# Turning the tokens' normalised rows by one DMA of four blocks instead of four TensorE transposes

## The chip, the core and the metric

The kernel runs on one core of one Trainium2 chip. The core has TensorE (PE in the profile, with PEld for its weight loads), VectorE (DVE), ScalarE (ACT), GpSimd (POOL) and SyncE (SP), which in this kernel issues nearly all DMAs. The engines run side by side, each with its own list of instructions that it takes strictly in order; they wait for each other by semaphores. The metric is the device time of one execution in microseconds (us); the kernel before has a median of 1510.49 us over 3 runs (1509.76 to 1510.58).

## The reference

Four layers follow each other on 2048 tokens of 448 features: attention with memory, a gated unit, the same attention with the same weights again, the same gated unit again.

```python
x = A_x
x = x + _A_ref(_layernorm(x), A_mem0, A_Wq, A_Wk, A_Wv, A_Wo, A_seg_len)
x = x + _B_ref(_layernorm(x), B_W_gate, B_W_up, B_W_down)
x = x + _A_ref(_layernorm(x), A_mem0, A_Wq, A_Wk, A_Wv, A_Wo, A_seg_len)
x = x + _B_ref(_layernorm(x), B_W_gate, B_W_up, B_W_down)

# _A_ref: 16 heads of 256; segments of 32 tokens, 8 memory rows in front of each
mem = mem0
for s in range(n_seg):                       # 64 segments, one after the other
    h = concat([mem, xs])                    # 40 rows
    q, k, v = h @ Wq, h @ Wk, h @ Wv
    p = softmax(where(mask, q @ k.T / 16, -1e9))
    o = (p @ v) @ Wo
    mem = o[:8]                              # the next segment's memory
    outs.append(o[8:])

# _B_ref
gate = x @ W_gate
out = (gate * (gate > 0) * (x @ W_up)) @ W_down
```

The memory makes a chain: a segment's 8 memory rows come out of the whole attention of the segment before it.

## The kernel before

**Weights.** Wq and Wk of a head are multiplied once into a matrix A (`self.A`, 448 x 448 a head), and Wv with Wo into B (`self.Bsb`). A score is then `h A h^T`, and the output `p h B`. TensorE spends about the first 118 us on that.

**Tiles, steps, layers.** Tokens are worked on in 16 tiles of 128 (four segments each). Each of the two attention layers (layer 0 and layer 1 in the code) has 64 segments. `program` runs over steps: at step `n`, `chain(n)` carries the memory rows of layer 0 from segment `n` to `n + 1`, and those of layer 1 from segment `n - 7` (`LAG`) on; both ride through the same matmuls. Up to two times eight query rows of layer 1's even tiles ride along too (`board` copies them into the chain's operand `mT`). Between the chain's parts, `tiles` lets TensorE do the rest of a tile's work: `att_group` four times (the matmuls with A, L1626; scores, L1655; softmax; `p h`, L1537 and L1541; B, L1693), then `glu_units` (L1715) and `glu_down` (L1733), for layer 0 and for layer 1.

**One step of the chain.** Matmuls with A (L1268), evictions into `Usb`, turning with a selection matrix (L1444), scores (L1467), softmax on ACT and DVE, the turn of P on TensorE into `PTm` (L1507), `p h` (L1534), evictions into `YTm`, matmuls with B (L1307), four partial sums added by ACT and DVE (L1322, L1324 twice, L1325) into `Ohi`, a small copy (L1205), and the turn of the new memory rows by matmuls with a selection (L1350), whose evictions fill `mT` for the next step.

**The rows that the change is about.** `norm(t, ("A", l))` makes a tile's normalised rows `xn` (128 tokens by 448 features): statistics (L1556, L1557), two small ACT operations (L1558, L1560), the scaling (L1562) and a copy of the first 64 features (L1205, in `twice`). Matmuls need these rows with the features on the partitions. 448 is three and a half times 128, so there are four blocks, the last of them holding 64 features twice. TensorE turns the four blocks (L1580) into one PSUM bank. From there one copy makes `HT`, where each segment's 32 columns have 8 more for its memory (stride 40), and two copies make `HX`, which holds the first three blocks with their halves of 64 partitions exchanged: the matmuls with A (L1626) work on 64 rows at a time, two side by side, and each side takes seven half blocks, four from `HT` and three from `HX`. The same norm issues eight small DMAs that put the rows, not turned, into `HR` (24 KB and 4 KB pieces). `HT`, `HX` and `HR` have two buffers for layer 0 and three for layer 1 (`NB`). For the gated unit (`norm(t, "G")`) the rows are turned by two DMAs from SBUF to SBUF already, of three and of four blocks (`turn_dma`, L1046), and softmax results of the tiles and of the riders as well.

**The order.** No scheduler runs at build time: `ORDER` is one long list, found by a search outside of this file, that holds each operation's number times five plus the number of its engine; each engine takes its operations in the list's order. `BANKS` gives the PSUM bank of each use. `FILLS` names places in that list at which TensorE gets matmuls without a use ("fillers", L183): number, bank, and shape. Each of them may start once `s.still` (a cleared tile, `warm`) is there.

```python
FILLS = {56: (11, 0, 0), 69: (9, 0, 0), 1306: (7, 2, 0), 1461: (46, 1, 1)}
```

Of the kernel before, what the change touches and what calls it, by code (L numbers as in the profile page):

```python
# [7 lines left out]
ALU = mybir.AluOpType  # L8
# [8 lines left out]
SEG = 32  # L17
# [267 lines left out]
def bass_interleave_layers__memory_aug_recurrent_mem_tr__glu_gated_reglu__prompt_kernel(  # L285
# [22 lines left out]
    206, 2, 8, 199, 211, 204, 22, 142, 78, 12, 226, 219, 138, 148, 231, 224, 246, 239, 17, 251, 244, 27, 32, 58,  # L308
    37, 153, 92, 266, 259, 42, 158, 102, 163, 47, 112, 271, 264, 275, 52, 168, 122, 290, 62, 173, 281, 639, 67, 178,
    297, 183, 539, 188, 286, 302, 193, 72, 305, 82, 2128, 544, 87, 320, 2133, 311, 549, 327, 316, 554, 332, 335, 559, 355,  # L310
    341, 564, 362, 569, 435, 643, 405, 574, 441, 420, 412, 669, 450, 446, 417, 426, 345, 674, 457, 385, 431, 462, 351, 879,
    495, 392, 525, 884, 501, 485, 532, 889, 375, 491, 365, 894, 382, 395, 371, 465, 899, 402, 515, 471, 904, 475, 522, 505,
    909, 481, 605, 512, 914, 95, 790, 611, 2167, 590, 1179, 797, 620, 616, 1184, 596, 105, 775, 2172, 802, 627, 575, 1189, 2176,
    632, 760, 601, 782, 2181, 1194, 581, 115, 645, 745, 2187, 652, 1199, 657, 2193, 586, 662, 751, 767, 735, 2204, 675, 772, 741,
    787, 695, 2209, 757, 682, 705, 701, 2214, 825, 2162, 712, 815, 2219, 831, 2157, 865, 2257, 821, 2224, 725, 872, 715, 731, 2229,
    805, 2262, 722, 2266, 845, 2234, 811, 685, 852, 2271, 2239, 855, 691, 2277, 835, 1204, 861, 960, 2282, 842, 1209, 1060, 966, 1075,
    1214, 1067, 1045, 971, 1072, 1081, 945, 1479, 1052, 1090, 951, 1057, 930, 1087, 1097, 915, 936, 1102, 957, 1115, 922, 1155, 941, 927,
    1121, 1484, 1125, 1162, 1105, 1559, 1131, 975, 1112, 1135, 981, 1165, 1142, 1005, 1171, 995, 1012, 1035, 1001, 1025, 1042, 1015, 1031, 1145,
    1022, 985, 1151, 1390, 1564, 992, 125, 1230, 1396, 132, 1639, 1375, 1237, 1260, 1401, 1242, 1381, 1515, 1267, 1360, 1386, 1272, 1525, 1366,
    1485, 1345, 1371, 1535, 1351, 1495, 1644, 1542, 1215, 1356, 1505, 1719, 1221, 1492, 1245, 1565, 1226, 1252, 1501, 1575, 1257, 1585, 1571, 1512,  # L320
    1435, 1521, 1582, 1445, 1531, 1295, 1442, 1591, 1625, 1452, 1301, 1405, 1415, 1411, 1724, 1305, 1422, 1285, 1799, 1311, 1455, 1292, 1335, 1461,
    1275, 1342, 1315, 1281, 1465, 1322, 1325, 1471, 1425, 1332, 1545, 1431, 1705, 1804, 1552, 2345, 1879, 2350, 2285, 2356, 2362, 1605, 2331, 1595,
    1612, 2195, 1601, 1735, 2242, 1665, 2336, 2247, 1745, 2252, 1741, 1615, 2342, 1645, 1884, 1751, 1622, 1675, 1651, 1959, 2365, 1632, 1681, 2370,
    1695, 2376, 2382, 2385, 1655, 2391, 1765, 1661, 1685, 1772, 1805, 1671, 1964, 1855, 1811, 1692, 1775, 2039, 1701, 1815, 1782, 1925, 1711, 1822,
    1935, 2395, 1905, 2401, 1835, 1911, 2405, 1825, 1842, 1941, 1755, 2412, 1915, 1831, 1725, 1861, 2415, 2044, 1865, 1732, 1945, 2139, 2422, 1871,
    1762, 2025, 2426, 2144, 1785, 1952, 1985, 2149, 1791, 2432, 2118, 2437, 2015, 1991, 2154, 1885, 1975, 2021, 2294, 1892, 2005, 1981, 2032, 1845,
    2299, 1921, 2440, 1965, 2012, 2123, 2304, 2446, 1895, 1851, 1972, 1995, 2309, 1901, 2055, 2002, 2314, 1931, 2045, 2062, 2065, 2319, 2051, 2075,
    2072, 2324, 2085, 2081, 4157, 2095, 2329, 2105, 2091, 2102, 2559, 2450, 2111, 4162, 2457, 2569, 2461, 3365, 6062, 4166, 3370, 2579, 4171, 4177,
    2465, 2584, 4182, 6067, 6071, 6076, 2490, 2471, 2564, 2477, 2483, 2574, 2487, 3375, 2496, 2589, 3380, 2502, 2594, 2505, 3386, 2510, 2515, 2522,
    2527, 2599, 2605, 3391, 2532, 2537, 2541, 2625, 2549, 2630, 2554, 2610, 2636, 2642, 3395, 2616, 2622, 2824, 2655, 2645, 2819, 2661, 2665, 3400,  # L330
    2651, 2672, 2829, 2675, 3405, 2682, 2604, 2686, 3530, 3412, 3535, 2692, 3417, 3426, 2697, 3421, 3432, 2700, 3540, 3437, 2706, 2710, 2839, 3545,
    2716, 2722, 3551, 2725, 2834, 3556, 2750, 2731, 2737, 2849, 2743, 2747, 2844, 3560, 2756, 3565, 2762, 2765, 2770, 2775, 2781, 2786, 2859, 2865,
    2791, 2797, 2801, 2870, 2809, 2885, 2814, 2876, 2882, 2854, 2890, 3079, 3570, 2896, 2902, 3695, 3576, 2905, 3084, 3581, 3592, 2915, 3586, 2925,
    3700, 2912, 2921, 2932, 2864, 3596, 3601, 2935, 3705, 2942, 3089, 2946, 3710, 2952, 3094, 3725, 2957, 3716, 3722, 2960, 3730, 2966, 2970, 3099,
    3735, 2976, 2982, 3741, 3757, 3104, 2985, 3746, 3762, 3751, 3767, 3010, 2991, 2997, 3109, 3003, 3007, 3860, 3016, 3025, 3022, 3030, 3035, 3041,
    3046, 3145, 3051, 3057, 3061, 3150, 3069, 3125, 3074, 3156, 3162, 3114, 3130, 3440, 3136, 3142, 3175, 3605, 3447, 3181, 3452, 3165, 3185, 3612,
    3865, 3171, 3192, 3457, 3195, 3617, 3870, 3461, 3202, 3622, 3206, 3875, 3467, 3626, 3212, 3890, 3472, 3119, 3217, 3881, 3477, 3220, 3632, 3895,
    3484, 3886, 3227, 3637, 3230, 3642, 3900, 3236, 3242, 3906, 3922, 3649, 3270, 3911, 3927, 3916, 3932, 3359, 3245, 3276, 3124, 3282, 3364, 3485,
    3251, 5510, 3491, 3257, 3263, 3267, 3496, 3650, 5516, 5522, 3500, 3285, 3290, 3506, 3770, 3339, 3657, 3301, 3295, 3306, 3512, 3311, 4275, 3321,
    3662, 3316, 3777, 4295, 3329, 3782, 3787, 3334, 4280, 3791, 3797, 4300, 4286, 4292, 3344, 3665, 3802, 4306, 4312, 4315, 3935, 3671, 4322, 3515,  # L340
    3807, 3676, 4248, 3942, 3814, 3947, 4253, 4335, 3952, 4258, 4325, 3520, 4342, 3956, 4263, 4332, 4999, 3962, 4268, 3967, 4273, 4345, 3525, 3972,
    5004, 4352, 4356, 3979, 3680, 4362, 4367, 4370, 3685, 3349, 4376, 4380, 3830, 4386, 4392, 3815, 3837, 3841, 4395, 3821, 3827, 4420, 4401, 3354,
    4407, 4413, 4417, 3690, 4426, 4432, 4435, 4440, 3980, 4451, 4456, 3995, 3987, 4194, 4485, 4461, 4471, 3991, 4002, 4199, 4490, 4006, 4204, 4505,
    4496, 4502, 4209, 4510, 4214, 4445, 4516, 4522, 4219, 3845, 4466, 4224, 4525, 4479, 4545, 4535, 4531, 3850, 4552, 4541, 4484, 4229, 4555, 3855,
    4562, 4566, 4010, 4572, 4577, 4580, 4015, 4586, 4590, 5385, 4596, 4602, 4605, 5391, 5407, 5396, 5412, 5401, 5417, 4630, 4611, 4617, 4623, 4627,
    4020, 4636, 4642, 4645, 4650, 4027, 4655, 4661, 4666, 4695, 4671, 4032, 4676, 4682, 4037, 4715, 4041, 4689, 4046, 4052, 4700, 4694, 4057, 4720,
    4064, 4706, 4712, 4726, 4732, 4735, 4741, 4069, 4745, 4755, 4185, 4751, 4762, 4231, 6082, 4765, 5370, 4772, 6088, 4236, 4776, 4242, 4782, 4787,
    4790, 5525, 5376, 5382, 4796, 4800, 5531, 5547, 4070, 8334, 4806, 4812, 5536, 5552, 5541, 5557, 4840, 4076, 4082, 4815, 4846, 4852, 8337, 8342,
    4085, 4821, 8346, 4827, 4833, 8351, 4837, 4130, 4091, 4097, 4855, 4860, 4100, 4871, 4876, 4881, 4891, 5012, 5560, 4106, 5420, 4112, 4115, 5427,
    5567, 4135, 5432, 4121, 5572, 5437, 4127, 5441, 4140, 5577, 5447, 5581, 5452, 4145, 5587, 5457, 5665, 4152, 5464, 5592, 4907, 5650, 5597, 5671,  # L350
    4912, 5687, 4916, 5604, 5676, 5692, 4921, 5697, 5681, 4927, 4865, 5656, 4932, 4944, 5662, 4935, 4886, 5790, 4949, 4982, 4987, 5018, 4899, 4992,
    4904, 5007, 5023, 5465, 5796, 5802, 5025, 4954, 5471, 5477, 4959, 5030, 4964, 5045, 5036, 5042, 4969, 5050, 4974, 5480, 5056, 5062, 6153, 5105,
    4979, 6158, 5700, 5486, 5112, 5069, 5115, 5491, 5125, 5707, 5605, 5122, 5620, 5611, 5805, 5132, 5616, 5627, 5631, 5712, 5135, 5717, 5811, 5495,
    5827, 5816, 5721, 5142, 5822, 5146, 5727, 5500, 5151, 5157, 5831, 5167, 5836, 5162, 5172, 5732, 5175, 5840, 5737, 5181, 5744, 5185, 5847, 5505,
    5191, 5197, 5071, 5077, 5082, 5200, 5852, 5089, 5857, 5861, 5867, 5225, 5872, 5206, 5877, 5212, 5884, 5217, 5635, 5222, 5252, 5231, 5237, 5640,
# [464 lines left out]
class _Kernel:  # L820
# [153 lines left out]
    def constants(self):  # L974
# [9 lines left out]
        def dve(fn, **k):  # L984
            s.add("dve", 250, lambda E, e: fn(E), **k)
# [875 lines left out]
```

## Time and profile before

| what | value |
|---|---|
| median of 3 runs | 1510.49 us |
| the profiled execution | 1517.04 us; span from its first to its last instruction 1515.3 us |
| mean granted TensorE clock | 0.997 |
| matmuls | 37579, of them 128 transposes in `norm` (L1580) and 73 fillers (L183) |
| busy: DVE, ACT, POOL | 1109.6, 841.0, 60.0 us |
| turning DMAs now | 64 into G, 96 into Tx, 124 into UR, 62 into Tr, 8 of weights |

Times in the views are microseconds from the span's start unless they are marked ns. Matmuls are pipelined: the duration of one reaches from its start to its modelled end, and the next ones start long before that, so a group's cost is read from the start of its first to the start of what comes after it. In a window's row stand length, then busy time and (in brackets) the instructions of PE, PEld, DVE, ACT and POOL, then the granted TensorE clock as a share of full speed, the DMA engines' busy share and GB/s. In a row of waits stand who waited, for whom, the sum, how often and the longest. In a timeline's row the square brackets hold the idle time of that engine just ahead of it and what ended it.

### The profile page before, as it was taken

What the parts mean: (1) busy time and instruction counts of PE and PEld (TensorE: products, weight loads), DVE (VectorE), ACT (ScalarE), POOL (GpSimd) and SP (SyncE); (2) the same over time, 40 slices, a digit from 0 to 9 for tenths busy, and PEclk for the clock granted to TensorE, in tenths of its full rate; (3) what the DMA queues carried; (4) which work ended last, traced back from release to release, by engine and by line L of the source; (5) the groups of instructions that cost most, each with busy time, mean ns of one, the idle gap of its engine ahead of it and who ended that gap; (6) DMA issues with size and microseconds to landing.
All of it is one profiled execution on the core that took longest, in us unless ns stands there. A gap on an engine that the chain in (4) does not pass through costs nothing.

```text
span 1515.3 us, 83381 instructions
## 1 busy us (share of the span) xinstructions
PE 1478.4 (98%) x37579; PEld 1063.1 (70%) x37579; DVE 1109.6 (73%) x3353; ACT 841.0 (56%) x2383; POOL 60.0 (4%) x240
## 2 busy tenths in 40 slices
PE   8999999999999999999999999999999999999998
PEld 6576766667667776677767777677767676677675
DVE  7655768678776878678776778778777878778774
ACT  6755556556565556555655655555555556545542
POOL 1000000000000000000000000000000000000000
PEclk9999999999999999999999999999999999999999
DMA  9831122222222212212122223213222222213211
GB/s 237 194 89 44 28 43 44 44 37 46 46 39 41 45 32 51 42 31 52 44 42 38 44 44 53 40 35 47 47 44 31 52 43 53 39 41 40 47 27 27
DMA packets 239346, 78.20 MB, mean 52 GB/s; under 512 B 212104, under 2 KB 238992, under 8 KB 238992
## 3 DMA queue, kind: packets, MB, share of 16 engines
q1 hardware_dynamic: 238352, 72.60, 25.2%
q8 instruction: 297, 4.87, 1.4%
q14 instruction: 57, 0.47, 0.1%
q10 hardware_dynamic: 640, 0.26, 0.1%
HBM read 17.68 MB, written 1.84 MB: 13 GB/s over the span
## 4 chain that ended last, share of the span: by engine, by line
PE 87%; DVE 6%; DMA 3%; ACT 2%; issue 1%; SPq 1%; DVEq 0%; POOL 0%
PE psG L1626 14%; PE psG L1693 14%; PE psG L1715 11%; PE psC L1307 11%; PE psC L1268 7%; PE psG L1733 6%; PE psG L1268 5%; PE psG L1104 3%; PE psG L1537 2%; PE psG L1655 2%; PE psC L1467 1%; PE psC L1693 1%; PE psC L1444 1%; DMA UR<-Usb 1%; PE psC L1534 1%
## 5 line engine op out<-in xcount | busy, mean ns | idle before, releaser
L1693 PE MATMUL psG<-Bsb,YT 128*128 128x448 bf16 x1232 | 263.8, 353 | 0.0
L278 ACT ACTIVATE Ug<-psG 64x128 bf16<-64x128 f32 (+2 forms) x424 | 152.7, 374 | 73.6 <-PE psG L1626 64.5
L1307 PE MATMUL psC<-Bsb,YTm 128*32 128x448 bf16 (+2 forms) x4088 | 188.0, 335 | 1.0 <-DVE YTm L281 0.5
L1715 PE MATMUL psG<-G,glu 64*128 64x128 bf16 x5866 | 183.6, 216 | 2.6 <-DMA G<-xn 2.4
L1715 PEld LDWEIGHTS psG<-G,glu 64*128 64x128 bf16 x5866 | 170.3, 94 | 14.5 <-issue 8.6
L1626 PE MATMUL psG<-HT,A 64*128 64x128 bf16 x3424 | 175.8, 217 | 0.3 <-ACT Bsb L278 0.3
L1693 PEld LDWEIGHTS psG<-Bsb,YT 128*128 128x128 bf16 x1232 | 107.3, 97 | 89.0 <-issue 7.7
L1268 PE MATMUL psG<-A,mT 64*32 64x448 bf16 x4564 | 158.8, 350 | 2.8 <-issue 1.9
L1626 PE MATMUL psG<-HX,A 64*128 64x128 bf16 x2568 | 149.9, 217 | 0.0
L1307 PEld LDWEIGHTS psC<-Bsb,YTm 128*32 128x32 bf16 x4088 | 101.4, 97 | 67.2 <-DVE YTm L281 3.2
L281 DVE CAST Ug<-psG 64x128 bf16<-64x128 f32 (+2 forms) x277 | 114.9, 427 | 25.3 <-PE psG L1626 21.3
L1268 PE MATMUL psC<-A,mT 64*32 64x448 bf16 x3276 | 128.8, 351 | 1.0 <-issue 0.6
L1626 PEld LDWEIGHTS psG<-HT,A 64*128 64x128 bf16 x3424 | 116.6, 94 | 8.9 <-issue 5.0
L1324 DVE TENSOR_TENSOR Usb<-psC,Usb 32x448 f32<-32x448 f32 (+2 forms) x122 | 74.4, 610 | 63.7 <-ACT Usb L1322 60.9
L278 ACT ACTIVATE YT<-psG 128x448 bf16<-128x448 f32 x217 | 109.3, 538 | 20.3 <-PE psG L1541 20.0
L281 DVE CAST YT<-psG 128x448 bf16<-128x448 f32 x145 | 88.2, 618 | 41.2 <-PE psG L1541 40.4
L1720 ACT ACTIVATE hG<-psG 128x512 bf16<-128x512 f32 (+1 forms) x123 | 66.7, 543 | 81.6 <-PE psG L1715 78.8
L1268 PEld LDWEIGHTS psG<-A,mT 64*32 64x32 bf16 x4564 | 80.5, 92 | 32.3 <-issue 4.0
L1733 PE MATMUL psG<-glu,hG 128*128 128x448 bf16 x448 | 99.8, 353 | 0.0
L1268 PEld LDWEIGHTS psC<-A,mT 64*32 64x32 bf16 x3276 | 64.9, 93 | 45.4 <-ACT mT L278 2.7
L1626 PEld LDWEIGHTS psG<-HX,A 64*128 64x128 bf16 x2568 | 95.2, 94 | 0.0
L1626 PE MATMUL psG<-l,A 64*128 64x128 bf16 x2807 | 94.4, 216 | 0.0
(274 smaller groups left out, 2755.7 us busy)
## 6 DMA issues: line engine op xcount, KB each, us to landing
Bsb<-in_A_Wq_dram SPq DMA_DIRECT2D x6, 384.0 KB
Bsb<-in_A_Wk_dram SPq DMA_DIRECT2D x6, 384.0 KB
Tsb<-Ohi SPq DMA_DIRECT2D x128, 7.0 KB
UR<-Usb SPq DMA_TRANSPOSE x124, 2.9
X<-in_A_x_dram SPq DMA_DIRECT2D x16, 112.0 KB, 5.6
glu<-in_A_Wo_dram SPq DMA_DIRECT2D x4, 448.0 KB
out_dram<-X SPq DMA_DIRECT2D x16, 112.0 KB
glu<-in_B_W_gate_dram SPq DMA_DIRECT2D x14, 112.0 KB
```

Of the source, the lines that this page charges most:

```text
L278: return E.activation(out, i, ACT.Copy, scale=1.0 if scale is None else scale)
L281: return E.tensor_copy(out, i)
L1104: i = E.matmul(bk.ap()[row0:row0 + mn, 0:D], lhsT=lhs[:, et, m0:m0 + mn], rhs=rhs[:, et, :], start=(et == 0), stop=(et == 1), tile_positio ...
L1268: i = E.matmul(ub[v].ap()[32 * j:32 * j + 32, 0:D], lhsT=self.mT[rw, b, :], rhs=self.A[rw, b, a0:a0 + D], start=(b == 0), stop=(b == 6), t ...
L1307: x = E.matmul(bo.ap()[32 * j:32 * j + 32, 0:d1 - d0], lhsT=self.YTm[:, q, :], rhs=self.Bsb[:, chunks[q], d0:d1], start=(i == 0), stop=(i ...
L1324: s.add("dve", dv_cost(n), lambda E, e, j=j, a_=a_, part=part: E.tensor_tensor(a_, part(j), a_, ALU.add), r=[bo], w=w, part=(j, 0), **P)
L1537: return E.matmul(ps[:, n * q:n * q + n], lhsT=HR[rows, KM + 128 * q:KM + 128 * q + 128], rhs=PT, start=True, stop=True, tile_position=(b, 0))
L1626: i = E.matmul(ub[v].ap()[:, 128 * n:128 * n + 128], lhsT=self.A[rw, b, a0:a0 + 128], rhs=HT[rw, b, :, 0:SEG] if b < 4 else HX[rw, b - 4, ...
L1693: i = E.matmul(bo.ap()[:, 0:D], lhsT=YT[:, c, :], rhs=self.Bsb[:, 14 * g + c, :], start=(g == 0 and c == 0), stop=(g == 3 and c == 13))
L1715: i_ = E.matmul(two[v].ap()[:, 128 * c:128 * c + 128], lhsT=self.Wgu[rw, b, f0:f0 + 128], rhs=G[rw, b, :], start=(b == 0), stop=(b == 6), ...
L1720: s.add("act", 169 + 0.84 * N, lambda E, e, dst=dst, z=two[0], N=N: E.activation(dst, z.ap()[:, 0:N], ACT.Relu), r=[two[0]], w=[("hG", i, ...
L1733: i_ = E.matmul(bk.ap()[:, 0:D], lhsT=hG[:, c, :], rhs=self.Wd[:, c, :], start=(c == 0), stop=(c == NFC - 1))
```

## The change

- `norm(t, ("A", l))` turns the rows by one DMA of four blocks into `HX`, which now has four blocks; the tail copy goes behind the rows instead of ahead of them. Tiles 0 and 1 of layer 0 keep the transposes on TensorE (with one more copy for each half).
- `HT` is then copied from `HX`, SBUF to SBUF: two half copies (three blocks, 64 partitions, on ACT or DVE) and two quarter copies (one block, 64 partitions; one on POOL, the other on ACT or DVE).
- The matmuls with A take three half blocks from `HT` and four from `HX`.
- `board` and `board_one` copy their part of `HX` in two halves, one on POOL and one on ACT or DVE.
- To make room, `warm` goes (fillers use `ident`, and wait for it), `lnst` and `stx` become parts of one tile, and `PTm` lies in the bytes of `Tm`.
- `ORDER`, `BANKS` and `FILLS` are new. The list has 9394 entries for 9295: 30 fewer on PE, 3 fewer on ACT, 76 more on DVE, 26 more on POOL, 30 more on SP. There are 175 fillers for 73.

```diff
-FILLS = {56: (11, 0, 0), 69: (9, 0, 0), 1306: (7, 2, 0), 1461: (46, 1, 1)}
+FILLS = {54: (17, 0, 0), 1287: (46, 1, 1), 1329: (8, 3, 0), 1469: (46, 1, 1), 1808: (12, 1, 1), 1915: (46, 1, 1)}
...
-            self.s.psum, self.s.ident = self.psum, self.warm
+            self.s.psum, self.s.ident = self.psum, self.ident
...
-        self.HX = [[part(l, f"HX{l}_{i}", 3 * 128).rearrange("p (a b) -> p a b", a=3) for i in range(NB[l])] for l in range(2)]
+        self.HX = [[part(l, f"HX{l}_{i}", 4 * 128).rearrange("p (a b) -> p a b", a=4) for i in range(NB[l])] for l in range(2)]
...
-        self.PTm = sb("PTm", [128, 128])
+        self.PTm = self.Tm.rearrange("p c k -> p (c k)").bitcast(BF)[:, 0:128]
...
# board (board_one alike)
-        self.s.add("pool", 225, lambda E, e: E.tensor_copy(self.mT[:, 4:7, 16:32].rearrange("p k (q a) -> p k a q", a=2),
-                                                           HX[:, :, :].rearrange("p k (g q) -> p k g q", g=4)[:, :, g:g + 2, o:o + 8]),
-                   r=[("HX", 1, b, 0), ("HX", 1, b, 1)], w=["mTr"], prio=0)
+        for v in range(2):
+            rw = slice(64 * v, 64 * v + 64)
+            self.s.add(("act", "dve") if v else ("pool",), {"pool": 225, "act": 240, "dve": 175},
+                       copy_any(self.mT[rw, 4:7, 16:32].rearrange("p k (q a) -> p k a q", a=2),
+                                lambda rw=rw, v=v: HX[rw, 1 - v:4 - v, :].rearrange("p k (g q) -> p k g q", g=4)[:, :, g:g + 2, o:o + 8]),
+                       r=[("HX", 1, b, 0), ("HX", 1, b, 1)], w=["mTr"], part=(2 * v, 2 * v), prio=0)
...
# norm
-        self.twice(xn, ("xn", i), ("xnt", i), dict(prio=prio))
-        bk = self.bank("G", "C")
...
-        s.add("pe", mm_cost(*[128] * 4), tr, r=xnk + ["ident"], w=[bk], alloc=[bk], room=[("HTx", l, b), ("HX", l, b, 0), ("HX", l, b, 1)], prio=prio)
+        hx = [("HX", l, b, 0), ("HX", l, b, 1)]
+        early = l == 0 and t < 2
+        if early:
+            self.twice(xn, ("xn", i), ("xnt", i), dict(prio=prio))
...
+        else:
+            s.add(("pool", "dve"), {"pool": 240, "dve": dv_cost(64, fast=True)},
+                  lambda E, e: E.tensor_copy(xn[:, XW:XW + 64], xn[:, 64:128]), r=[("xn", i)], w=[("xnt", i)], prio=prio)
+            self.turn_dma(HX[:, :, :], xn[:, 64:XW + 64], 131072, r=xnk, w=hx, prio=prio)
...
+        if not early:
+            for v in range(2):
+                rw, z = slice(64 * v, 64 * v + 64), slice(64 - 64 * v, 128 - 64 * v)
+                s.add(EV, {"act": 523, "dve": 251}, copy_any(HT[rw, 0:3, :, 0:SEG], lambda z=z, v=v: HX[z, v:v + 3, :].rearrange("p k (g q) -> p k g q", g=4)),
+                      r=hx, w=[("HTx", l, b)], part=(2 - 2 * v, 2 * v), prio=prio)
+                s.add(("act", "dve") if v else ("pool",), {"pool": 300, "act": 290, "dve": 190},
+                      copy_any(HT[rw, 3, :, 0:SEG], lambda rw=rw, v=v: HX[rw, 3 * v, :].rearrange("p (g q) -> p g q", g=4)),
+                      r=hx, w=[("HTx", l, b)], part=(2 * v, 2 * v), prio=prio)
+            return None
...
# att_group
-                                         rhs=HT[rw, b, :, 0:SEG] if b < 4 else HX[rw, b - 4, :], start=(b == 0), stop=(b == 6), tile_position=(64 * v, 0))
+                                         rhs=HT[rw, b, :, 0:SEG] if b < 3 else HX[rw, (b - 3, (3, 0, 1, 2)[b - 3])[v], :], start=(b == 0), stop=(b == 6), tile_position=(64 * v, 0))
```

## The prediction

> **What bounds the kernel now.** I read the page's shares first, then the chain that ended last.
>
> ```profile
> PE 1478.4 (98%) x37579; PEld 1063.1 (70%) x37579; DVE 1109.6 (73%) x3353; ACT 841.0 (56%) x2383; POOL 60.0 (4%) x240
> PE 87%; DVE 6%; DMA 3%; ACT 2%; issue 1%; SPq 1%; DVEq 0%; POOL 0%
> ```
>
> TensorE is busy for 1478.4 of 1515.3 us. Of the 36.9 us that are left, 5.5 lie before its first matmul and 4.8 after its last, so some 26.6 us are holes inside. A change can gain by taking work from TensorE or by closing holes, and it loses by opening holes; what happens on the other engines counts only through holes.
>
> Then the timeline of TensorE around one turned tile:
>
> ```profile
> 1103.66 0.35 PE L1268 MATMUL psC<-A,mT 64*32 64x448 bf16 x1
> ...
> 1103.85 0.35 PE L1268 MATMUL psG<-A,mT 64*32 64x448 bf16 x1
> 1104.14 0.40 PE L1580 MATMUL psG<-ident,xn 128*128 128x128 bf16 x4
> 1104.37 0.34 PE L1444 MATMUL psC<-Selm,Usb 128*128 128x64 bf16 x6
> ```
>
> Matmuls overlap, so the price is read from start to start. The four transposes (L1580) hold TensorE from 1104.14 to 1104.37, 0.23 us. The second price is the change of tiling: rows of L1268 follow each other after 0.19 us (1103.66, 1103.85), but the first 128*128 matmul comes 0.29 us after the last 64*32 one, so a change of shape costs about 0.10 us.
>
> Last, the holes, by windows (PE busy; the column after POOL is the granted clock) and by TensorE's waits from 186 to 333 us, the chain's steps 7 to 15:
>
> ```profile
> 286.00:309.00 23.00, 18.41 (x495) 12.55 (x483) 15.52 (x45) 9.53 (x26) 0.24 (x1) 1.00 0.20 38
> 309.00:316.00 7.00, 6.37 (x128) 5.44 (x136) 4.45 (x20) 3.32 (x11) 0.50 (x2) 0.51 0.08 20
> 316.00:333.00 17.00, 16.96 (x479) 12.62 (x464) 13.50 (x38) 10.20 (x30) 0.50 (x2) 1.00 0.33 43
> PE psC L1350 <- DVE Ohi L1205: 2.2, 2, 2.0
> PE psG L1715 <- DMA G<-xn: 2.2, 1, 2.2
> ```
>
> After two holes of 2.2 and 2.0 us the clock is at half for about 7 us, though TensorE is then busy for 6.37 of 7.00: about 3.4 us are lost. The second hole is a step's tail:
>
> ```profile
> 305.86 0.53 ACT L1322 ACTIVATE Usb<-psC 32x448 f32<-32x448 f32 x1 [0.68 <-PE psC L1307]
> 306.43 1.27 DVE L1324 TENSOR_TENSOR Usb<-psC,Usb 32x448 f32<-32x448 f32 x2 [0.60 <-ACT Usb L1322]
> 308.18 0.62 DVE L1325 TENSOR_TENSOR Ohi<-psC,Usb 32x448 bf16<-32x448 f32 x1
> 308.84 0.18 DVE L1205 COPY Ohi<-Ohi 128x64 bf16<-128x64 bf16 x1
> 309.08 0.27 PE L1350 MATMUL psC<-Sel,Ohi 64*128 64x16 bf16 x4 [1.99 <-DVE Ohi L1205]
> ```
>
> 0.53 + 1.27 + 0.62 + 0.18 and the gaps between make 2.8 us that TensorE must fill with other work at each step's end.
>
> **TensorE's work.** Tiles 0 and 1 of layer 0 keep their transposes; 30 of 32 groups go: 30 x 0.225 = -6.8 us. ORDER holds five times the operation's number plus the engine's, so the new order can be laid beside the old one. In it TensorE changes shape 570 times against 552: 18 x 0.10 = +1.8. Fillers are taken as cover of holes below. Work: **-5.0 us**.
>
> **The evictions.** For those 30 tiles ACT loses 35 half copies of 485 ns and 19 whole ones of 595 (28.3 us), DVE 25 of 355 and 11 of 419 (13.5). Added, as ORDER assigns them, with the nearest rows (uTr<-UR, 128x384: 519 on ACT, 249 on DVE; 64x64: 248 and 172): 36 half copies on ACT and 24 on DVE; 12 quarter copies on ACT, 18 on DVE, 30 on POOL at about 240; 24 half boards on ACT, 42 on DVE. ACT 18.7 + 3.0 + 6.0 = 27.7, DVE 6.0 + 3.1 + 7.2 = 16.3: no change on engines with 44% and 27% free. POOL's 7 us lie on an engine at 4%. If DVE's 2.8 us had no cover they would cost 2.8. Reading block 3 from HX is free: L1626 takes 217 ns with HT and with HX.
>
> **The turn itself.** Its nearest row is the same transfer into G:
>
> ```profile
> L1046 SPq DMA_TRANSPOSE G<-xn x64: 1178/1265/2457, 146.5 to 1497.4; - x64
> DMA to landing us min/median/max: 2.5/2.5/2.9
> ```
>
> So 30 x 1.27 = 38 us more of SP's issuing, which now is about 354 turns x 1.25 + 749 others x 0.6 = 890 us of 1515; behind a turn wait the tile's eight row copies (0.59 us each), needed only after scores and softmax. Per tile the turn puts 2.5 + 0.52 us where transposes and eviction took 0.4 + 0.6: 2.0 us more latency. From glu_down's last matmul of a tile to the first matmul that needs layer 1's rows the way is add_x 0.62, statistics 0.62 + 0.18, ACT 0.29 + 0.20, scaling 0.39, tail copy 0.24, turn 2.5, copy 0.52, board 0.25: 5.8 us. Adding up the durations of the matmuls that the new order puts between the two gives 9.5 us at the least (tile 0) and 10.5 to 24 elsewhere; the old order had 5.6 at the least. From the turn's own place to that matmul (2.5 + 0.52 + 0.25 = 3.3 needed) it has 5.1 at the least, in layer 0 6.1. Hidden: **0**, with 1.8 us to spare where it is tightest. Layer 1's tiles 1 and 2 are the ones to watch: six row copies, 3.6 us of issuing, stand before their turns on SP, against one at most in the other 14. If SP gets late by more than the 1.8 us, holes open: end of the range +10 (rival three).
>
> On the choice of path the Trainium skill, page "VectorE: DVE Perf Modes", sections "The three transpose paths" and "Rules for kernel authors", speaks against the change: 390 ns for a 128x128 on TensorE, 1309 ns by DMA, so TensorE where PSUM will do. The latencies here agree in direction (0.4 against 2.5 us for four blocks); that rule prices latency, and by it the time would be that of the fourth rival below.
>
>
> **The holes.** In the old order the tails of steps 8, 10 and 14 have a hole of 0.6, 46 fillers (2.5 us) and a hole of 2.0. The new order has 46 fillers, and nothing else, in all three: 2 x 2.8 - 0.6 - 2.0 = +3.0. Twelve fillers at step 13 stand where the 2.2 us wait for G stood: 0. A tail in step 11 lacks 0.5 of its 2.8, and two evictions in steps 5 and 6 have no matmuls between their ends: +1.0. From step 16 on I count the old holes again. Sum **+4.5 us** (bounds 0, if the fillers only cover what was open before, and +9, if all 102 new fillers at 54 ns, 5.5 us, come on top of every old hole and another 3.5 opens).
>
> **The clock.** Fillers keep TensorE running in three of these holes, so the half clock should stay away: **-3.4 us** (bounds -3.4 and 0). The Trainium skill, page "TensorE: Matmul & The Clock Gate", section "Part 1: The HAM clock gate (the "warmup" mystery)", states that the clock is halved after an idle window of about 3.4 us. The trace differs: no hole there was over 2.3 us. By the page those holes were not the cause and this term is 0: rival two.
>
> **No cost:** PTm in Tm's bytes (Tm's next writer comes a step, 16 us or more, after PTm's last reader); `ident` for `warm` (the first transposes need it anyway); `small` (only an address).
>
> **Sum:** -5.0 + 4.5 - 3.4 = -3.9 us. The profiled execution took 1517.04 us (span 1515.3), 6.5 above the runs' median; none of the terms grows with that, so 1513.1 for a like profile and 1506.6 for the median.
>
> **Rivals.**
> 1. Holes do not grow: the fillers stand in holes that the old order had as well (it had 2.2, 2.0, 0.6 open). For it: the positions coincide; against: step 8's tail was nearly covered. -8.4: 1502.1.
> 2. The half clock stays, or is not in unprofiled runs to begin with. For it: the page's rule, and that one execution shows it; against: the drop follows the two holes at once. -0.5: 1510.0.
> 3. Slower: the in-order queues. 60 half copies stand on ACT and DVE and wait there for a landing. If SP issues a turn late, behind one other turn (1.25 us) or row copies, the engine stops with the chain's evictions behind it, and these are what TensorE waits for. 0.33 us of it for each of 30 turns is 10 us: -3.9 + 10 = +6.1, 1516.6. It decides from 0.23 us for a turn (6.9 / 30). For it: SP is at 59%; against: G's landings vary only from 2.5 to 2.9, and only two of layer 1's turns have more than one row copy before them.
> 4. The latency is not hidden at all: 16 layer-1 tiles x 2.0 = +32, less 3.9: 1538.6. It decides only where a tile's cover, 9.5 us or more, falls under the way's 5.8. The skill's rule above leads here.
>
> **Chances.** About 0.2% (3.0 us) is what a measurement of this kernel can tell from no change. Forecast 0.40 (as it lies only 0.9 us past that bound: faster 0.27, same 0.13); rival one 0.13 (faster); two 0.20 (faster 0.02, same 0.14, slower 0.04); three 0.22 and four 0.05 (slower). Together faster 0.42, same 0.27, slower 0.31. The range, 1499 to 1518, leaves out the fourth, and the far ends of the first and third; the forecast's own is 1503 to 1510.
>
> **What would show it.** L1580's group at 8 matmuls instead of 128. A window at each 46-filler with L1350 starting within 0.5 us of the last filler: a longer wait there means that step tails are dearer than 2.8. PEclk at 1.00 in every window from 16 to 1500 us: if 0.5 shows again, the clock term fails. HX<-xn landing in 2.5 us. TensorE's holes inside near 26.6 + 4.5 - 5.5 (the new fillers count as busy) = 26 us. ACT and DVE rows waiting for "DMA HX<-xn" by over 7 us in all would speak for rival three; waits of L1268 or L1467 for HT copies in layer 1, for rival four.

## The result, and the profile after

The changed kernel takes 1524.63 us in the median of four runs (1522.72 to 1527.02), against 1510.47 for the kernel before on the same chip: a ratio of 1.0096, 95% interval 1.0078 to 1.0113, 14.2 us slower. The profiled execution took 1527.02 us; its span, 1525.2, is 9.9 us longer than that of the profiled one of before. The kernel before spreads more than these runs show: over the 86 executions that came with the experiments, on five chips, it lies between 1507.3 and 1520.2 us, and on one chip by up to 9.9 us. The 9.9 us that the two traces show and the 14.2 of the medians differ by less than that spread, so I take them as one loss. Medians below are compared by their ratio to the runs of before on the same chip.

The page's shares and the chain that ended last:

```profile
PE 1483.7 (97%) x37561; PEld 1061.3 (70%) x37561; DVE 1123.1 (74%) x3429; ACT 844.2 (55%) x2380; POOL 67.6 (4%) x266
PE 85%; DVE 8%; DMA 3%; ACT 2%; issue 1%; SPq 1%; POOL 0%; DVEq 0%; POOLq 0%
```

TensorE is busy for 5.3 us more, although it has fewer matmuls, and idle for 41.5 us instead of 36.9. The turned tile is gone from its list, but for the two early tiles. The first row below is TensorE's; the second is that of the new turn in layer 0, with the least, median and longest duration on SP in ns (layer 1's 16 turns are printed with `l` for `HX`):

```profile
L1594 PE MATMUL psG<-ident,xn 128*128 128x128 bf16 x8 | 0.8, 219 | 0.0
```

```profile
L1048 SPq DMA_TRANSPOSE HX<-xn x14: 1195/1261/1914, 112.0 to 1276.7; - x14
```

The stretch of the chain's steps 7 to 15, TensorE's waits:

```profile
PE psC L1541 <- DMA Tr<-Pr: 1.9, 1, 1.9
PE psC L1541 <- ACT uTr L278: 1.3, 1, 1.3
PE psG L1740 <- issue: 1.2, 1, 1.2
...
PE psC L1352 <- DVE Ohi L1207: 0.8, 3, 0.3
```

and its windows (granted clock after POOL):

```profile
290.00:318.00 28.00, 25.76 (x699) 20.17 (x689) 20.92 (x70) 11.78 (x37) 0.00 (x0) 1.00 0.20 35
318.00:323.40 5.40, 3.46 (x126) 3.29 (x122) 3.79 (x11) 2.58 (x6) 0.78 (x3) 1.00 0.19 40
323.40:327.00 3.60, 3.60 (x90) 2.03 (x92) 1.08 (x4) 1.16 (x5) 0.00 (x0) 0.53 0.41 75
```

The tails of these steps are covered now (L1352 waits 0.3 at most, where it was 2.0). But there are new holes, of 1.9 and 1.3 us, both ahead of L1541, which needs the riders' turned P (`Tr<-Pr`); and the half clock is back behind the larger one. The second hole's row names ACT's copy `uTr`, which ended at 252.32; by the trace P had landed only 0.1 us before that. What stood ahead of that P on SP is in the timeline (a layer-1 tile of `HX` lies in the tile `l2`, printed `l`):

```profile
316.75 1.70 SPq L1048 DMA_TRANSPOSE l<-xn  x1
...
318.49 1.23 SPq L1048 DMA_TRANSPOSE Tr<-Pr  x1
...
322.51 0.40 PE L1541 MATMUL psC<-Tr,l 40*128 40x128 bf16 x10 [1.94 <-DMA Tr<-Pr]
```

A new turn of a tile's rows holds SP for 1.70 us, P's turn comes next, and TensorE idles 1.94 us for it. The late issue is not all of it: from the start of P's turn to the matmul it is 4.0 us, where the five turns into `Tr` whose landing the trace of before could tell took 2.3 to 3.5, 2.4 in the median. So some 1.6 us are a slow landing, and whether the turn ahead caused that is not shown. The hole from 251.07 us on has a like history: a new turn at 243.88, then three row copies and a turn into `UR` without a pause on SP, and P's turn only at 249.41.

From TensorE's first to its last matmul it takes 9.6 us more. Counted from start to start, of that are work -6.8 us, 19 more changes of shape +1.85 and 102 more fillers +5.5. The rest, +9.0, is waits, with the half clock within it (3.4 us lost before, 1.7 after). Some 4 us of it can be seen as idle time between matmuls (26.6 us before, 30.8 now); the rest lies inside the modelled durations.

### The profile page after: what moved, and what is told of

Same layout as the page of the kernel before. It is cut to its first block, busy times and chain, and to the rows that moved or that the text cites. A ratio compares the mean times of both kernels' runs of the same rounds, so it can differ in the third digit from the quotient of the medians.

```text
span 1525.2 us, 83452 instructions
## 1 busy us (share of the span) xinstructions
PE 1483.7 (97%) x37561; PEld 1061.3 (70%) x37561; DVE 1123.1 (74%) x3429; ACT 844.2 (55%) x2380; POOL 67.6 (4%) x266
## 4 chain that ended last, share of the span: by engine, by line
PE 85%; DVE 8%; DMA 3%; ACT 2%; issue 1%; SPq 1%; POOL 0%; DVEq 0%; POOLq 0%
PE psG L1718 15%; PE psG L1651 13%; PE psC L1309 11%; PE psG L1740 11%; PE psC L1270 8%; PE psG L1758 5%; PE psG L1270 5%; PE psG L1106 3%; PE psG L1544 2%; PE psG L1680 2%; PE psC L1474 1%; PE psC L1451 1%; DMA UR<-Usb 1%; DVE Usb L1326 1%; PE psC L1541 1%
## 5 line engine op out<-in xcount | busy, mean ns | idle before, releaser
L1718 PE MATMUL psG<-Bsb,YT 128*128 128x448 bf16 x1344 | 288.2, 353 | 0.0
L1718 PEld LDWEIGHTS psG<-Bsb,YT 128*128 128x128 bf16 x1344 | 116.2, 97 | 102.3 <-issue 13.5
L278 ACT ACTIVATE Ug<-psG 64x128 bf16<-64x128 f32 (+2 forms) x406 | 148.3, 382 | 61.2 <-PE psG L1651 48.0
L1651 PE MATMUL psG<-HX,A 64*128 64x128 bf16 x3248 | 169.6, 216 | 0.0
L1270 PE MATMUL psC<-A,mT 64*32 64x448 bf16 x3556 | 146.7, 353 | 1.8 <-ACT mT L278 1.2
L1651 PE MATMUL psG<-HT,A 64*128 64x128 bf16 x2436 | 146.5, 217 | 0.3 <-ACT Bsb L278 0.3
L281 DVE CAST Ug<-psG 64x128 bf16<-64x128 f32 (+2 forms) x258 | 105.9, 423 | 20.1 <-PE psG L1651 15.4
L1651 PEld LDWEIGHTS psG<-HX,A 64*128 64x128 bf16 x3248 | 117.0, 94 | 0.0
L1270 PEld LDWEIGHTS psC<-A,mT 64*32 64x32 bf16 x3556 | 73.0, 93 | 51.8 <-issue 5.0
L1651 PEld LDWEIGHTS psG<-HT,A 64*128 64x128 bf16 x2436 | 89.3, 94 | 7.2 <-issue 3.5
```

What stands on the lines that cost most here:

```text
L278: return E.activation(out, i, ACT.Copy, scale=1.0 if scale is None else scale)
L281: return E.tensor_copy(out, i)
L1270: i = E.matmul(ub[v].ap()[32 * j:32 * j + 32, 0:D], lhsT=self.mT[rw, b, :], rhs=self.A[rw, b, a0:a0 + D], start=(b == 0), stop=(b == 6), t ...
L1651: i = E.matmul(ub[v].ap()[:, 128 * n:128 * n + 128], lhsT=self.A[rw, b, a0:a0 + 128], rhs=HT[rw, b, :, 0:SEG] if b < 3 else HX[rw, (b - 3, ...
L1718: i = E.matmul(bo.ap()[:, 0:D], lhsT=YT[:, c, :], rhs=self.Bsb[:, 14 * g + c, :], start=(g == 0 and c == 0), stop=(g == 3 and c == 13))
```

## Experiments

### The orders crossed

Theories: the new order costs the time, or the turn does. Where tiles go back to TensorE, their transposes and evictions are put into the new order by hand.

```diff
# new_order_pe: ORDER, BANKS, FILLS of the changed kernel
-        early = l == 0 and t < 2
+        early = True
# old_order_turn, old_order_l0: ORDER, BANKS, FILLS of before; second halves of the boards on DVE
# old_order_l0
-        early = l == 0 and t < 2
+        early = l == 1 or t < 2
# old_order_15: copies put by hand into gaps of ACT and DVE
+        early = (l, t) not in ((0, 2), (0, 3), (0, 4), (0, 5), (1, 5), ...)
```

> The new order, banks and fillers, but all 32 tiles turned by TensorE: the 30 turning DMAs and the copies HX to HT go, 30 groups of four transposes with their evictions out of PSUM come back, each just ahead of the place of the first copy. Theory 'order' (the 14.2 us come from the new order; the DMA itself saves its 6.8 us of TensorE): 1524.6 + 6.8 = about 1531, 1527 at the least. Theory 'turn' (the DMA, with SP's issuing, its latency and the added copies, costs what the kernel lost, about 7.5 us of longer waits spread over steps 20 to the end, and the order only 7): 1524.6 - 7.5 + 6.8 = about 1524, and if the turn is dear, less: 1517 to 1524.

Measured: 1569.76 us, ratio 1.0381 (1.0356 to 1.0406).

> The old order, banks and fillers with the change's turn: 30 tiles turned by DMA, issued as soon as the rows are ready, copies in the places of the old evictions, second halves of the boards on DVE. Theory 'order': 1510.5 - 6.8 = about 1504, up to 1508. Theory 'turn': above 1515; where layer 1's rows come too late for the old places (2.0 us more latency for 16 tiles) up to 1540.

Measured: 1563.36, ratio 1.0327 (1.0302 to 1.0352).

> The old order with only layer 0's 14 tiles (2 to 15) turned by DMA; layer 1's 16 and layer 0's tiles 0 and 1 stay on TensorE. Layer 0's rows are not needed by the chain at once, so latency is out, SP's issuing stays (14 x 1.26 us). Theory 'order': 1510.5 - 14 x 0.225 = about 1507. Theory 'turn' by SP and the added copies: 14/30 of 7.5 us of waits, less 3.2: about 1511 to 1515. If only the latency on layer 1's side costs: about 1507 here and over 1515 with all 30.

Measured: 1544.67, ratio 1.0204 (1.0185 to 1.0224).

> The old order with 15 tiles turned by DMA: those whose rows are ready 8.9 us or more before the first instruction that uses them in the trace of before; the other 17 stay on TensorE. The turn goes on SP ahead of what follows when the rows are ready, the copies into gaps of ACT and DVE 4 us or more later. Theory 'the turn is good where it has room, the old order hadn't the room elsewhere': 15 x 0.225 = 3.4 us less than before, ratio 0.998, 0.996 to 1.000. Theory 'each turn costs through SP's queue, the added copies and DVE, room or not' (14.2 us and the 6.8 of TensorE for 30): 15 x 0.47 = 7 us more, ratio 1.005, 1.003 to 1.010.

Measured: 1540.71, ratio 1.0176 (1.0153 to 1.0198).

Neither theory in this form stands: every mixture of one order with the other way of turning is dearer than both kernels. For one part the traces say why. From the end of the tail copy to the first instruction that reads `HT` or `HX`, the old order leaves 6.4 us or less for 11 of the 30 tiles (1.1 at the least), the new one 5.4 at the least. The new order pulls norms and users apart. But the run with 15 tiles that have 8.9 us or more lost too, 26.7 us. So something other than the turn's own latency costs; these kernels also carry the split boards and, for tiles left on TensorE, two more evictions each. That called for one part at a time.

### The turn alone

The kernel before, with 30 turns that nothing reads:

```diff
+        if l or t > 1:
+            self.turn_dma(self.scratch[:, :, :], xn[:, 0:XW], 131072, r=xnk, w=[], prio=prio)
...
         s.add("pe", mm_cost(*[128] * 4), tr, ...)
# extra_turns_small
+            self.turn_dma(self.scratch[:, 0, :], xn[:, 0:128], 32768, ...)
# extra_turns_gaps: 20 of the turns later in ORDER, where SP idled; extra_gaps_20: only these 20; extra_none: no turn
```

> The kernel before, complete with its TensorE transposes, plus 30 turning DMAs of four blocks (a tile's rows xn into a scratch tile that nothing reads), each issued by SP right behind the tail copy. It is the turn's load on SP and on the DMA engines alone: no copies, no latency, no new order. Theory 'SP's queue': leaving out 64 us of issuing gave 6.7 us, 0.105 us for 1; so 30 x 1.26 = 38 us of issuing cost about 4.0 us, ratio 1.0026, 1.001 to 1.005. Theory 'the turn is free, the rest costs': 1.000 within 0.001. If a turn holds SP longer than a row copy in a worse place: 1.007 or more, half of the whole loss.

Measured: 1538.42, ratio 1.0159 (1.0139 to 1.0179): 24 us, six times the 4.0 expected from the price of a row copy.

> The 30 extra turns in their first places, but of one block (32 KB) instead of four. A one-block turn (Tr<-Pr) holds SP for 1.14 us in the trace of before, one of four blocks for 1.26. Theory 'SP's queue': 0.9 of 24 us, ratio 1.014, 1.012 to 1.017. Theory 'DMA work': a quarter of it, 6 us, ratio 1.002 to 1.006.

Measured: 1535.09, ratio 1.0152 (1.0133 to 1.0171). A quarter of the bytes, the same cost. The turn's rows, first in this run and then in the run with four blocks, agree with that: one block holds SP about as long as four.

```profile
L1056 SPq DMA_TRANSPOSE scratch<-xn x30: 1119/1226/2379, 71.9 to 1425.6; - x30
```

```profile
L1056 SPq DMA_TRANSPOSE scratch<-xn x30: 1188/1262/2525, 72.0 to 1429.3; - x30
```

> The kernel with the 30 extra turns that nothing reads, but 20 of them issued later, in stretches in which SP was idle for 1.5 us or more in the trace of before (1 to 27 us after the rows are ready); the other 10, all of layer 0, come 1 to 6 us after the rows are ready, with no idle stretch in reach. Theory 'a turn costs what it delays on SP where it is issued': 20 of 30 at nothing, so 8 to 10 us, ratio 1.005 to 1.008. Theory 'a turn costs by the DMA engines' work and reading the rows, wherever it is issued': 1.0159 again, 1.013 or more.

Measured: 1529.09, ratio 1.0112 (1.0094 to 1.0131), 17 us: twice what was expected of the ten that stayed.

> Only the 20 extra turns that stand in idle stretches of SP; the 10 of layer 0 that were issued within 6 us of their rows are gone. Theory 'a turn costs what it delays on SP where it is issued': 1 to 5 us, ratio 1.001 to 1.003, and the 10 tight ones cost 12 to 16 us, over 1 us each. Theory 'every transposing DMA on the queue costs the same': 20/30 of 17, 11 us, ratio 1.0075.

Measured: 1514.02, ratio 1.0002 (0.9988 to 1.0015). Twenty turns in idle stretches of SP cost nothing.

> The kernel of the extra turns with none of them: only the edits that make room (fillers use ident, the small statistics tiles joined, a scratch tile that is never used) and the order before. Theory 'these edits cost nothing': 1.000 within 0.0015. If they cost: 1.003 or more, and the 24 us of the extra turns shrink by it.

Measured: 1514.60, ratio 1.0005 (0.9992 to 1.0018). The edits that made room cost nothing.

So ten turns, all of layer 0 from its tile 6 on, make up nearly the whole 17 us. The run with 30 turns, 20 of them in gaps, and the run with those 20 alone have the same TensorE instructions in the same order, so their k-th matmuls can be set against each other. From the first of the ten on the first run falls behind by 13.5 us, 13.4 of it within 15 us behind those ten turns, from 0.2 less to 3.7 more at one. SP's timeline at the dearest one, first without and then with the turn:

```profile
1190.98 0.62 SPq L1061 DMA_DIRECT2D Tsb<-Ohi  x1
1191.65 6.80 SPq L1061 DMA_DIRECT2D HR<-xn  x8
1198.49 1.30 SPq L1056 DMA_TRANSPOSE UR<-Usb  x1
1199.84 1.24 SPq L1056 DMA_TRANSPOSE Tr<-Pr  x1
```

```profile
1199.66 0.62 SPq L1061 DMA_DIRECT2D Tsb<-Ohi  x1
1200.33 2.12 SPq L1061 DMA_DIRECT2D HR<-xn  x2
1202.55 1.23 SPq L1056 DMA_TRANSPOSE scratch<-xn  x1
1203.82 4.88 SPq L1061 DMA_DIRECT2D HR<-xn  x6
1208.75 1.30 SPq L1056 DMA_TRANSPOSE UR<-Usb  x1
1210.09 1.23 SPq L1056 DMA_TRANSPOSE Tr<-Pr  x1
```

and what follows on DVE and TensorE in the second:

```profile
1210.42 0.40 DVE L1572 TENSOR_SCALAR xn<-X,small 128x448 bf16<-128x448 bf16 x1 [2.18 <-DMA HR<-xn]
...
1210.94 0.24 DVE L1494 TENSOR_SCALAR Pm<-Tm,stm 128x40 bf16<-128x40 f32 x1
```

```profile
1211.58 0.23 PE L1517 MATMUL psC<-ident,Pm 128*128 128x128 bf16 x1 [2.07 <-DVE Pm L1494]
```

The eight row copies end on SP at 1208.70 instead of 1198.45, 9.04 and 7.47 us behind the start of `Tsb`. They are the last readers of `xn`; the scaling of a later tile into that buffer (L1572) stands in DVE's line and waits 2.18 us for them; behind it stands the chain's P (`Pm`), and for that TensorE idles 2.07 us. SP has no pause in which to catch up: adding up its rows in the trace of before, it issues for 95% of the 15 us after each of these ten norms, for 75% after layer 1's, and for 66% of the whole span. A turn there pushes back all that comes behind it.

The riders' other turned tile, `UR`, shows the same in sums. These are ACT's waits for it before, with the 30 extra turns, and with the twenty in idle stretches:

```profile
ACT uTr L278 <- DMA UR<-Usb: 11.9, 11, 2.6
ACT uTr L286 <- DMA UR<-Usb: 29.3, 22, 2.6
ACT uTr L286 <- DMA UR<-Usb: 15.2, 13, 2.4
```

With DVE's they are 17.4, 47.8 and 22.2 us; in the changed kernel they are 23.2.

### SP relieved

```diff
# after_less_rows, before_less_rows
+                if t < NB[l]:
                     self.dma(H[64 * h:64 * h + SEG, KT:KT + 64], xn[r0:r0 + SEG, 64:128], 8192, ...)
# after_rows_pool, before_rows_pool: the same copy (before_rows_pool_all: the 24 KB one as well)
-                self.dma(H[...], xn[...], 8192, ...)
+                s.add("pool", 60, lambda E, e, ...: E.dma_start(H[...], xn[...]), ..., dma=8192, prio=prio)
```

> The changed kernel with 108 fewer DMAs on SP: the small piece (64 columns) of the row copies into HR is left out for all tiles after the first use of each buffer, so those columns hold an older tile's values. SP has 108 x 0.59 = 64 us less to issue, against 38 us that the turns added. Theory 'SP's queue makes the turns and the riders late': 5 to 9 us less than the changed kernel, ratio to before 1.004 to 1.006. Theory 'DVE' or 'order': within 2 us of it, 1.008 to 1.011.

Measured: 1522.30, ratio 1.0051 (1.0032 to 1.0069).

> The kernel before with the same 108 small row copies left out. It tells what the relief of SP is worth without the turns. Theory 'SP's queue is where the turns cost': 0 to 2 us less than before, ratio 0.9985 to 1.0. If SP was as much in the way before: 5 us less or more, 0.997 or under, and the gain of the changed kernel says nothing on the turns.

Measured: 1509.94, ratio 0.9956 (0.9942 to 0.9971). Both kernels leave out 108 copies, so parts of `HR` hold older tiles' rows. Both gain about 7 us: SP was in the way before the change as well, so this pair alone doesn't say what the turns cost. Nor do the changed kernel's holes close: in the trace of `after_less_rows` TensorE idles 1.8 us for the riders' P at 253 us, again behind a new turn, three row copies and a turn into `UR`, and 6.83 us of half clock follow.

> The kernel before with 128 of its 256 row copies into HR (the pieces of 64 columns) issued by POOL instead of SP; nothing is left out. SP loses 128 x 0.59 = 76 us of issuing. Theory 'SP's queue is in the way': about 7 us less, ratio 0.994 to 0.997, if POOL (60 us busy of 1515) takes them without holding up the boards that it copies. If POOL's issuing is slow or its boards come late: 1.000 to 1.010.

Measured: 1505.94, ratio 0.9954 (0.9940 to 0.9968). This version does all the work and beats both kernels. POOL issues a row copy in 0.50 us (instructions | busy, mean ns of one):

```profile
L1594 POOL DMA_DIRECT2D HR<-xn x64 | 31.6, 500 | 42.8 <-DVE lnst L1559 21.6 <-PE psG L1543 14.9 <-PE psC L1543 6.0
```

> The changed kernel with the 128 small row copies (64 columns) issued by POOL instead of SP, nothing left out; the same edit gave the kernel before 6.9 us (ratio 0.9954). Theory 'SP's queue': 7 to 9 us less than the changed kernel, ratio to before 1.004 to 1.005. If POOL, which now also has half boards and quarter copies that wait for landings, is held up: 1.008 or more.

Measured: 1516.81, ratio 1.0032 (1.0022 to 1.0043): 9.7 us less than the changed kernel (1.0096 - 1.0032). The kernel before gained 6.9 by the same edit, and the 2.8 between the two are not clear of the intervals. ACT's and DVE's waits for `UR` fall from 23.2 to 8.5 us, and TensorE's idle time from 41.5 to 34.5. From 186 to 333 us its longest waits and those of the steps' tails now read:

```profile
PE psG L1546 <- DMA Tx<-Px: 1.5, 1, 1.5
PE psG L1546 <- ACT Tm L280: 0.9, 2, 0.5
PE psC L1354 <- DVE Ohi L1209: 0.8, 3, 0.3
```

Both holes ahead of the riders' P are gone, and with them the half clock at 323 us. A hole of 1.5 us for a softmax turn stands there instead, and a stretch of half clock of the same length comes at 639 us.

> The kernel before with all 256 row copies issued by POOL (0.50 us of POOL each, from the profile of the run with 128). SP loses 152 us of issuing. Theory 'SP's queue': 10 to 14 us less than before, ratio 0.991 to 0.994. If the first half took nearly all of the wait, or the boards behind POOL's issuing come late: 0.995 to 0.998.

Measured: 1507.47, ratio 0.9967 (0.9953 to 0.9981). The second half of the relief adds nothing that can be told from the noise.

### DVE and the small copies

```diff
# before_split_boards_dve (both board helpers)
-        self.s.add("pool", 225, lambda E, e: E.tensor_copy(self.mT[:, 4:7, ...], HX[:, :, ...]), ...)
+        for v in range(2):
+            self.s.add(("act", "dve") if v else ("pool",), ..., copy_any(self.mT[rw, 4:7, ...], HX[rw, :, ...]), ...)
# after_dve_less: ORDER only; 42 second halves and 18 quarter copies DVE -> ACT, 16 tail copies DVE -> POOL
```

> The kernel before with one part of the change alone: each board's copy out of HX in two halves of 64 partitions, the first on POOL as before, the second on DVE in the same place of the list (66 operations of 0.19 us, 12.5 us of DVE). Theory 'the added small operations stand in DVE's order ahead of the chain's evictions': 5 to 15 us more, ratio 1.003 to 1.010. Theory 'DVE has 27% free, only SP matters': 1.000 to 1.001.

Measured: 1519.55, ratio 1.0043 (1.0029 to 1.0058): 6.5 us for 66 copies of 0.19 us.

```profile
L281 DVE COPY mT<-l 64x48 bf16<-64x48 bf16 x62 | 12.1, 195 | 5.0 <-POOL mT L281 3.1
```

The 5.0 is DVE standing idle ahead of them in its order, mostly for the first half on POOL, with later work queued behind. An engine with 27% free time is not free where it stands in line.

> The changed kernel in its own order, with 76 small operations off DVE: 42 second halves of the boards and 18 quarter copies go to ACT, 16 tail copies to POOL (DVE loses about 14 us, ACT gains about 16). Theory 'DVE is the queue that makes TensorE wait': 3 to 6 us less than the changed kernel, ratio to before 1.005 to 1.008. Theory 'SP is': no change, 1.0096 within 0.002. If ACT is as tight as DVE: slower, 1.012 or more.

Measured: 1537.47, ratio 1.0144 (1.0123 to 1.0166), 7 us slower than the changed kernel. The theory missed as it was put. Sixty copies went to ACT and sixteen to POOL at once, and which of the two moves cost the 7 us was not taken apart; nor does the run tell how much of the changed kernel's loss is DVE's.

### Fillers and the clock

```diff
# after_first_filler
+FILLS = {54: (17, 0, 0)}
# before_fill2
+FILLS = {56: (11, 0, 0), 69: (9, 0, 0), 1306: (7, 2, 0), 1461: (46, 1, 1), 1797: (40, 7, 1), 1906: (36, 7, 1)}
```

> The changed kernel with the 17 fillers at the start only; the five later groups (158 fillers, 8.6 us at 54 ns) go. Theory 'fillers on top' (they delay matmuls that were ready): 1524.6 less 3 to 8, 1517 to 1522. Theory 'fillers are cover': the holes open in their place, 1524.6 within 1.5; and if the half clock then comes at more than one place, 3.4 us more for each, 1528 to 1532.

Measured: 1530.37, ratio 1.0105 (1.0085 to 1.0124), not to be told from the changed kernel's 1.0096. So here the fillers are cover, not load. Where 46 of them stood, a hole of 2.8 us opens, and the half clock follows (hole and stretch behind it, three times; a fourth stretch comes at 1130 us, 1.5 us behind a hole of 1.8):

```profile
205.00:207.80 2.80, 0.05 (x4) 0.00 (x0) 2.46 (x7) 1.05 (x2) 0.12 (x1) 1.00 0.45 95
207.80:212.00 4.20, 4.10 (x100) 2.12 (x108) 1.78 (x10) 1.19 (x6) 0.00 (x0) 0.59 0.06 12
238.60:241.40 2.80, 0.00 (x1) 0.00 (x1) 2.39 (x7) 0.92 (x3) 0.00 (x0) 1.00 0.22 46
241.40:246.00 4.60, 4.29 (x108) 2.25 (x116) 0.40 (x4) 0.95 (x6) 0.00 (x0) 0.63 0.06 14
311.10:314.00 2.90, 0.08 (x5) 0.04 (x2) 2.13 (x6) 0.53 (x1) 0.00 (x0) 1.00 0.08 19
314.00:321.00 7.00, 6.45 (x128) 6.00 (x128) 4.20 (x19) 2.76 (x12) 0.00 (x0) 0.51 0.16 34
```

> The kernel before with fillers in the two holes ahead of its stretch at half clock: 40 ahead of the matmuls that wait for G at 287 us, 36 in the tail of step 14 at 307 us. Theory of the prediction's clock term: the half clock is gone, 3.4 us less, ratio 0.998, clock 1.00 throughout. Rival: the half clock comes all the same, or is in few runs: 1.000 within 0.001. If the fillers delay: up to 1.001.

Measured: 1516.84, ratio 1.0025 (1.0012 to 1.0038), 3.8 us slower. In its trace the half clock at 309 us is gone as planned. But 3.41 us of it come at 568 us instead, 1.4 us behind a hole of 2.3 us for the riders' P. Matmul by matmul it is 4.4 us ahead of before at 350 us, 2.3 of which it has already at 280, ahead of the first new filler; at 1200 it leads by 4.8, then it loses 5.8 by 1450, with a hole of 1.8 us ahead of L1715 at 1209 that before hasn't. So the early gain did not last in this run. Why it was lost there was not pursued.

## Why the prediction was wrong

Forecast 1506.6 with a range to 1518; measured 1524.6.

**Work: right.** 120 transposes are gone, -6.8 by their price, and +1.85 for 19 changes of shape where 18 were counted.

**The turn itself, "Hidden: 0": the step that failed.** Its readers are indeed not kept waiting: in the changed kernel the waits that name a landing of `HX` add up to 0.2 us (DVE, once), and the 1.8 us to spare sufficed. The 2.5 us to landing were optimistic, though: only four of the 64 landings in `G` could be told, and the 30 extra turns, which could all be told, landed after 3.4 us in the median and 4.2 at most. But the step asked only who waits for the turn. It left out who stands behind it on SP: riders' turns, softmax turns, row copies. It had the 38 us of issuing, and set them against SP's mean load, "SP is at 59%"; SP's rows in the trace of before add up to 66%, and to 95% where it mattered. Alone, those turns cost 24 us in the old order, where the term had 0. The twenty in idle places cost nothing; the ten in full ones cost 1.3 us each by the traces and 1.7 by the medians, near the 1.27 that a turn holds SP. In the changed kernel the two largest holes inside stand behind new turns, and both are gone when POOL issues half of the row copies, while the one at 251 us stays when 108 copies are left out. POOL's help takes 9.7 us off, but off the kernel before it takes 6.9 as well.

**The evictions, "no change": wrong in the old order.** There split boards alone cost 6.5 us; inside the changed kernel they were not measured. "If DVE's 2.8 us had no cover they would cost 2.8" looked at the sum of busy time and not at waits in line.

**Holes, +4.5: mis-sized.** Fillers 5.5 and waits, with the clock taken out, about 10.7 (9.0 + 1.7) make 16. The three tails came out as predicted, but the stretches beside them did not: by the ends of the steps, 3.7 us are lost already at step 7 (186 us), ahead of the stretch that the prediction worked through. "From step 16 on I count the old holes again" failed too: all of the 9.9 us is there by step 20 (426 us), and after it the 22 groups of transposes that are still saved, 22 x 0.225 = 5.0 us, are on balance eaten by longer waits. The holes inside, forecast near 26 us, are 30.8.

**Clock, -3.4: half of it came.** A hole moved and the half clock with it; 1.7 of the 3.4 us lost remained. The Trainium skill's rule of an idle window of about 3.4 us (page "TensorE: Matmul & The Clock Gate", Part 1) doesn't describe these runs either: three holes of 2.8 us and one of 1.9 were each followed by half clock. Rival two leant on that rule. Its reason fails, as half clock did follow holes that short, but its doubt of the gain was sound: filling the two holes in the old order made nothing faster.

**Rivals.** The third had the right place, SP's queue, and the nearest time, 1516.6, yet less than half of the loss (6.1 of 14.1 us). Its mechanism was copies that hold ACT and DVE until the turn's own late landing, and the sign that it named for this, waits for `HX<-xn` of over 7 us, stayed at 0.2. What the runs show is that the turn makes other transfers late: ACT and DVE then stop for `UR` and TensorE for the riders' P, and in the runs with extra turns DVE for the row copies as well. The first fell: holes grew. The second is no nearer on the clock term, of which half stayed, than the forecast is, and missed the time. The fourth had the direction, but its mechanism, readers that wait, is excluded for the new order by those 0.2 us.

**What stays open.** The parts were measured in the old order: turns +24.0, boards +6.5, transposes -6.8, together +23.7, and the changed kernel lost 14.2. That the new order saved the difference is an inference, since parts need not add up. How the 14.2 divide between SP, the lists of DVE and ACT, and the new order itself inside the changed kernel was not settled: with half of the row copies on POOL it is still 0.8% above the kernel before with the same relief (1.0032 against 0.9954). Not tried: turning only the twenty tiles that have an idle place on SP, on top of the row copies on POOL.

## What to carry over

Before adding a DMA, sum up what its issuing engine does in the 15 us after the place where it goes, and name what is queued behind it; a share of the whole span hides it (66% on average, 95% at the ten places that cost 17 us). The same holds for a small copy on an engine with free time: price it by its wait in line, and look first for work that can leave the crowded queue (128 row copies from SP to POOL: 6.9 us) before adding to it. The Trainium skill (page "DMA: Bandwidth & Descriptors", section "Rules for kernel authors") says that spreading DMAs over issuing engines only saves sequencer issue time; here that time was the scarce one.

## Not expected of the hardware

- A transposing DMA from SBUF to SBUF of one 128x128 block holds SP for 1.23 us in the median, one of four blocks for 1.26; a plain row copy 0.59 on SP and 0.50 on POOL.
- Half-clock stretches last 3.41 or 6.83 us in the clock records of these runs, apart from the last one of each run, which the end of the kernel cuts off. Most come within 3 us behind a hole of 1.5 to 2.8 us, but in the changed kernel with its small row copies on POOL one came behind two holes of 0.5 and 0.6 us within 1.5 us, and the 2.2 us hole of before at 287 us had none of its own. In the trace of `extra_none`, which has the matmuls of before in their order, the hole of 1.99 us at 306 us brought no half clock either. So the length of a single hole doesn't decide.
- Executions of the kernel before spread by up to 9.9 us on one chip and by 12.9 over five (1507.3 to 1520.2), more than several of the edits cost.
